# A fused attention and rational feed-forward kernel: its hand-held issue list is replaced by another list of the same tokens

## The chip, the cores and the metric

The program runs on one core of one Trainium2 chip. The metric is the time of the program on the device in microseconds (us), a median over several runs. The engines named here are TensorE (PE in the rows; PEld is its weight load), VectorE (DVE), ScalarE (ACT), GpSimd (POOL) and SyncE (SP), which issues most of the DMA transfers. Each engine runs its own instructions in the order in which the program was written, and waits for the others by semaphores.

## The reference

The first half is an attention between 512 rows of `x` and 32 states, in both directions, for 8 batches and 8 heads of width 64. The result of both directions is one list of 4,352 tokens (8 batches of 512 + 32) of width 512, which goes through a feed-forward layer whose activation is a quotient of two polynomials. All of it is float32.

```python
scores = scale * np.matmul(x, state.transpose(0, 1, 3, 2))      # softmax over 32 states
xread = np.matmul(a, state)
scores2 = scale * np.matmul(state, x.transpose(0, 1, 3, 2))     # softmax over 512 rows
sread = np.matmul(a2, x)
...
h = x @ w_in                                                     # 512 -> 2048
P = a[0] + a[1] * h + a[2] * h2 + a[3] * h3
Q = 1.0 + np.abs(b[0]) * np.abs(h) + np.abs(b[1]) * h2
g = P / (Q + 1e-06)
return (g @ w_out).astype(np.float32)                            # 2048 -> 512
```

## The kernel before

The work is cut into 72 iterations: iteration n takes batch n // 8 (9 "batches": the 8 real ones with 512 rows each, and a last one, n = 64 to 71, with the 256 rows that `sread` made, so half as wide) and the slice n % 8 of the hidden width (256 of 2048 columns). The product of `xread` with `w_in` is folded: the small matrix state times w_in is formed once (tokens `X`, function `extra`, line 695, small tiles of 64 x 32), split into a high and a low float32r part, and multiplied with the softmax weights `a` (token `F`, function `front`, line 785). A float32 product is made of float32r products of high and low parts: three for `F`, and for the output (function `mm`, line 857) two with the high part of g (`mh`) and one with the low part (`ml`).

One iteration has these steps: `F` writes h into one of two PSUM banks that a ring shares (TensorE); `FC` and `FB` make two linear forms of h (ScalarE, lines 797 and 804); `mu`, `po`, `qd` (VectorE, lines 808, 812, 818) read h from PSUM and build both polynomials; `qa`, `ln`, `ex` (ScalarE, lines 824, 894, 904) make the reciprocal of the denominator as the exponential of a logarithm; `g1` (VectorE, line 829), which needs `ex`, writes the high part of g, and `g2`, `g3` (lines 835, 841) with `gl` (GpSimd, line 848) the low part. `mh` and `ml` add to four output banks, which `fl` copies out after 8 iterations and `os` stores. For n of 8 to 63 the folded matrix comes back from DRAM: `lm` loads it (SyncE), `fs` rounds it (ScalarE, line 740), `ft` takes the rest (GpSimd, line 744). The attention of the next batch (`scores`, `tr1`, `row_max`, `e2_T`, `e2_copy`, `sread` and others) runs between the iterations.

In the first 100 us the weights come in as 64-bit words and are turned into float32: `lr` loads a half (SyncE, buffers `raw` and `raw_w`), `cp` and `jr`, `jl` convert it (ScalarE line 300, VectorE lines 309 and 320). `lx` loads the next piece of `x`, `lc` the six coefficients, `ls` the states, and `pre` puts ScalarE's table set in place.

Which engine does what is fixed by these tokens. The order of every engine's work is set by the list `ORDER` alone: the program walks through it from front to back and calls the function of each token, and no scheduler changes that order afterwards.

```python
with tc.manual_schedule():
    for name, args in tokens:
        ops[name](*args)
...
"pre": lambda: nc.scalar.preload_act_table_set("natural_log_exp_and_others"),
"gl": lambda n: fourth(n, nc.gpsimd),
"gv": lambda n: fourth(n, nc.vector),
```

Of the kernel before, what the change touches and what calls it, by code (L numbers as in the profile page):

```python
# [23 lines left out]
    "lx ls:0:2 lc pre lx scores0:0 scores0:1 sc_copy0:0 sc_copy0:1 row_T0:1 col_max:0 row_T0:0 lr:0:0 "  # L24
    "cp:0:0 lr:0:1 jr:0 cp:0:1 row_max0:0 lr:1:0 ls:2:8 cp:1:0 jl:0 X:1 row_max0:1 row_sub0:1 "
    "row_exp0:1 X:0 row_sub0:0 row_exp0:0 XA:1 lr:1:1 cp:1:1 lr:3:0 jr:1 X:2 row_sum0:0 row_norm0:0 "
    "col_scale:0 col_exp:0:0 e2_T0:0 XA:0 fh:0 row_sum0:1 col_exp:0:1 lr:2:0 fo:0 XA:2 a_T0:0 a_hi0:0 "
    "row_norm0:1 jl:1 a_T0:1 lr:2:1 a_hi0:1 cb cv X:4 lr:4:0 lr:4:1 cp:2:0 cp:2:1 a_lo0:0 lr:3:1 XA:4 "
    "a_lo0:1 F:0:0 jr:2 F:0:1 jl:2 fh:1 cp:3:0 fo:1 F:1:0 lx F:1:1 lx cp:4:0 b0a jr:3 col_eps:0 "
    "cp:3:1 jr:4 FB:0 FC:0 jl:3 wh:3 wl:3:0 lr:5:0 wl:3:1 lr:5:1 FB:1 qd:0 qa:0 ln:0 ex:0 mu:0 qd:1 "  # L30
    "po:0 ws:1 e2_T0:1 e2_copy0:0 e2_copy0:1 sread:0:0 sread:0:1 cp:5:0 jr:5 cp:5:1 FC:1 g1:0 qa:1 "
    "mh:0:2 xs:1 g2:0 col_norm:0 sr_copy:0 g3:0 xs:0 lr:7:0 lr:7:1 ln:1 sr_T:0 sr_fin:0 cp:4:1 ws:0 "
    "ex:1 mu:1 po:1 X:5 XA:5 gl:0 jl:5 wh:5 wl:5:0 jl:4 lr:8:0 g1:1 X:8 XA:8 fh:2 cp:7:0 cp:7:1 "
    "mh:0:0 ml:0:0 fo:2 lr:6:0 lr:6:1 xs:5 jr:7 lr:9:0 xs:2 X:9 lr:8:1 g2:1 xs:4 jl:7 wl:5:1 XA:9 "
    "F:2:0 F:2:1 FC:2 FB:2 X:6 cp:6:0 lr:11:0 g3:1 lr:9:1 mh:0:1 jr:6 XA:6 xs:6 ml:0:1 qd:2 cp:6:1 "
    "jl:6 wh:7 qa:2 mu:2 po:2 gl:1 mh:0:3 mh:1:3 ws:2 ln:2 ex:2 ml:1:0 X:12 g1:2 XA:12 fh:3 wl:7:1 "
    "fo:3 xs:8 ml:0:2 cp:8:0 cp:8:1 cp:9:0 cp:9:1 ml:0:3 mh:1:0 jr:9 X:10 XA:10 ml:1:1 lr:10:0 F:3:0 "
    "F:3:1 FC:3 X:16 g2:2 wl:7:0 mh:2:2 jr:8 xs:9 FB:3 XA:16 mh:1:1 lr:11:1 xs:12 jl:9 ws:3 xs:10 "
    "wh:9 g3:2 jl:8 lr:10:1 mh:2:0 gl:2 fh:4 qd:3 qa:3 ln:3 mu:3 mh:1:2 ex:3 mh:2:3 ml:1:2 fo:4 "
    "lr:12:0 lr:12:1 X:13 po:3 g1:3 XA:13 xs:13 wl:9:0 X:14 XA:14 xs:14 cp:11:0 cp:11:1 jr:11 g2:3 "  # L40
    "wl:9:1 ml:2:2 cp:10:0 jr:10 cp:10:1 F:4:0 F:4:1 FC:4 ml:1:3 jl:11 FB:4 g3:3 gl:3 cp:12:0 mh:2:1 "
    "X:20 fh:5 XA:20 lr:13:0 wh:11 lr:13:1 jl:10 mh:3:3 xs:16 qd:4 fo:5 qa:4 xs:20 ml:2:3 mh:3:1 ln:4 "
    "ex:4 F:5:0 lr:14:0 F:5:1 FC:5 ml:3:2 cp:12:1 mu:4 po:4 ws:4 X:17 XA:17 lr:14:1 wl:11:1 wl:11:0 "
    "cp:13:0 jr:13 g1:4 jr:12 lx lx ml:3:1 ml:3:0 g2:4 g3:4 mh:3:2 cp:13:1 FB:5 X:21 XA:21 xs:21 "
    "jl:12 qd:5 qa:5 ln:5 ml:3:3 mh:4:1 mh:4:0 mh:4:3 ws:5 cp:14:0 mu:5 mh:3:0 jr:14 ex:5 po:5 jl:13 "
    "cp:14:1 g1:5 X:25 XA:25 gl:4 scores:1:0 scores:1:1 sc_copy:1 wh:13 ml:2:0 jl:14 ml:4:3 ml:4:0 "
    "wl:13:1 xs:17 g2:5 X:29 col_max:1 X:24 XA:29 fh:6 wl:13:0 ml:2:1 ml:4:1 lr:15:0 tr1:1 mh:4:2 "
    "wh:14 xs:25 col_scale:1 fo:6 F:6:0 col_exp:1:0 lr:15:1 row_max:1 cp:15:0 cp:15:1 F:6:1 g3:5 "
    "wl:14:0 mh:5:2 XA:24 gl:5 row_sub:1 FB:6 qd:6 X:28 row_exp:1 ml:4:2 row_sum:1 row_eps:1 "
    "row_norm:1:0 xs:29 jr:15 mh:5:1 row_norm:1:1 XA:28 col_exp:1:1 fh:7 lm:8 mh:5:3 xs:28 ml:5:3 "  # L50
    "FC:6 fs:8 qa:6 ln:6 fo:7 mh:5:0 lw:0 mu:6 po:6 ws:7 xs:24 ml:5:0 F:7:0 tr2:1 ex:6 g1:6 g2:6 "
    "a_hi:1 ml:5:1 ml:5:2 ft:8 jl:15 X:3 F:7:1 wl:14:1 mh:6:1 XA:3 g3:6 FB:7 col_eps:1 lm:10 FC:7 "
    "e2_T:1 mu:7 qd:7 lx lx gl:6 mh:6:2 lw:1 e2_copy:1 mh:6:0 wh:15 wl:15:1 fs:10 wl:15:0 sread:1:0 "
    "sread:1:1 col_norm:1 sr_copy:1 mh:6:3 ml:6:1 sr_T:1 ml:6:0 po:7 ml:6:3 qa:7 a_lo:1 lm:9 F:8:0 "
    "ln:7 sr_fin:1 ex:7 g1:7 F:8:1 FC:8 g2:7 ml:6:2 g3:7 mh:7:2 mh:7:1 fs:9 ft:9 mh:7:3 mh:7:0 F:9:0 "
    "FB:8 qd:8 qa:8 xs:3 ln:8 ex:8 F:9:1 FC:9 mu:8 po:8 g1:8 gl:7 ml:7:1 ml:7:2 fl:7:2 ft:10 fl:7:1 "
    "ml:7:3 fl:7:3 g2:8 g3:8 gl:8 F:10:0 F:10:1 FB:9 qd:9 FB:10 FC:10 mh:8:3 lm:12 ml:7:0 fl:7:0 "
    "fs:12 ft:12 lx qa:9 ln:9 lm:11 mh:8:1 fs:11 mh:8:2 ws:6 mu:9 po:9 ml:8:1 ml:8:2 F:12:0 F:12:1 "
    "mh:8:0 os:7:3 ex:9 mu:10 lm:13 qd:10 FB:12 po:10 ml:8:3 g1:9 ml:8:0 mh:9:1 mh:9:3 mh:9:0 ft:11 "
    "g2:9 g3:9 FC:12 F:11:0 F:11:1 mu:12 po:12 qa:10 gl:9 ml:9:1 lm:14 lx ln:10 ex:10 ml:9:2 FC:11 "  # L60
    "g1:10 mh:10:2 mh:10:0 fs:13 mh:10:3 FB:11 mh:10:1 qd:12 qa:12 ln:12 g2:10 ml:9:0 ex:12 X:7 g3:10 "
    "XA:7 qd:11 mh:9:2 qa:11 gl:10 ml:10:1 mu:11 ft:13 po:11 scores:2:0 scores:2:1 ln:11 g1:12 g2:12 "
    "sc_copy:2 tr1:2 ex:11 lw:3 X:15 fs:14 lw:6 mh:12:1 F:13:0 F:13:1 col_max:2 g1:11 XA:15 mh:12:0 "
    "g2:11 g3:11 row_max:2 FC:13 ml:10:3 os:7:2 lw:2 FB:13 mh:12:2 qd:13 ft:14 ml:9:3 lm:16 "
    "col_scale:2 lm:15 fs:15 row_sub:2 mh:11:3 xs:15 X:11 ml:10:2 XA:11 mh:11:0 lw:5 gl:11 g3:12 "
    "mu:13 po:13 row_exp:2 ml:11:2 ml:10:0 qa:13 row_sum:2 row_eps:2 gl:12 mh:12:3 ln:13 ex:13 F:14:0 "
    "F:14:1 FC:14 ml:11:0 ft:15 g1:13 mh:11:1 FB:14 qd:14 fs:16 col_exp:2:0 row_norm:2:0 ml:11:3 "
    "mh:11:2 mu:14 col_exp:2:1 g2:13 g3:13 qa:14 F:15:0 F:15:1 ml:12:1 ml:11:1 mh:13:0 FC:15 ml:12:3 "
    "po:14 lm:17 fs:17 ln:14 ex:14 mh:13:1 row_norm:2:1 tr2:2 mh:13:3 e2_T:2 FB:15 ml:12:2 g1:14 "
    "g2:14 mh:13:2 e2_copy:2 gl:13 ml:13:3 ml:13:2 a_hi:2 a_lo:2 mh:14:2 ml:12:0 ft:16 F:16:0 F:16:1 "  # L70
    "FC:16 FB:16 g3:14 mh:14:3 mh:14:0 lm:18 gl:14 ml:14:3 ml:14:1 lx mu:15 po:15 ml:14:2 qd:15 qa:15 "
# [957 lines left out]
```

## Time and profile before

| what | us |
|---|---|
| median of 3 runs (673.9 to 674.11) | 674.07 |
| the profiled execution | 675.09 |
| its span, first to last instruction | 673.3 |
| TensorE busy in the span | 650.9 |
| VectorE busy in the span | 629.3 |
| ScalarE busy | 521.7 |
| GpSimd busy | 307.8 |

The profiled execution took 1.8 us more than its span, and 1.0 us more than the median. The share of busy time of TensorE counts matmuls from the issue of each to its modelled end, so that two neighbours overlap; how dense they stand is read from the distance between their starts. The granted clock was 0.992 of full speed over the span.

### The profile page before, as it was taken

To read this page: it belongs to the slowest core of one execution; us is meant where nothing else is said; L and a number is where in the kernel's file an instruction comes from. 1 tells how busy PE (TensorE), PEld (TensorE's weight loads), DVE (VectorE), ACT (ScalarE), POOL (GpSimd) and SP (SyncE) were. 2 spreads that over 40 slices of the span, in tenths; PEclk is the share of its full clock that TensorE was granted. 3 is DMA by queue.
4 is the path that set the end of the run, shared out by engine and by line. 5 is a ranking of instruction groups with operands and counts; after the bars stand their busy time and mean duration, and the time that the engine had idled before them with its cause. 6 is when DMAs were issued, how large, how long until landed. Compare 5 with 4: busy or idle time off the path is not lost.

```text
span 673.3 us, 11301 instructions
## 1 busy us (share of the span) xinstructions
PE 650.9 (97%) x4474; PEld 509.5 (76%) x4474; DVE 629.3 (93%) x583; ACT 521.7 (77%) x633; POOL 307.8 (46%) x174
## 2 busy tenths in 40 slices
PE   4699999999999999999999999999999999999997
PEld 2466667877877777878878878778778788788895
DVE  4999999899999898999999999999999999998886
ACT  4989989887978788878687777877786868777473
POOL 0234446534644545363544355443554444544540
PEclk9979999999999999999999999999999999999999
DMA  8979887343066164044232210412220311203301
GB/s 329 373 253 356 297 285 251 110 142 127 17 180 210 48 215 149 29 134 140 85 107 88 91 48 17 139 49 77 95 79 17 125 33 47 64 31 94 91 21 47
DMA packets 30679, 85.67 MB, mean 127 GB/s; under 512 B 3490, under 2 KB 3618, under 8 KB 30626
## 3 DMA queue, kind: packets, MB, share of 16 engines
q1 hardware_dynamic: 30290, 84.56, 36.9%
q8 instruction: 35, 0.57, 0.4%
q10 hardware_dynamic: 336, 0.39, 0.3%
q14 instruction: 18, 0.15, 0.1%
HBM read 57.15 MB, written 27.79 MB: 126 GB/s over the span
## 4 chain that ended last, share of the span: by engine, by line
PE 41%; DVE 34%; ACT 11%; issue 9%; POOL 2%; DMA 1%; SPq 0%; DVEq 0%; POOLq 0%; ACTq 0%
PE h L785 13%; DVE gh L829 7%; DVE C L808 5%; DVE A L818 5%; DVE A L835 5%; DVE C L812 3%; DVE C L841 3%; PE ps_x L695 2%; POOL gl L848 2%; PE o__5821 L857 2%; PE o__5809 L857 2%; ACT A L824 1%; ACT cv_y L300 1%; ACT C L797 1%; DVE aT L500 1%
## 5 line engine op out<-in xcount | busy, mean ns | idle before, releaser
L848 POOL TENSOR_TENSOR gl<-C,L 128x1024 fp32r<-128x1024 f32 (+1 forms) x70 | 176.0, 2516 | 255.1 <-DVE C L841 164.9
L785 PE MATMUL h<-aT,m 128*128 128x512 f32 x768 | 188.8, 392 | 1.3 <-DVE m L731 0.6
L785 PEld LDWEIGHTS h<-aT,m 128*128 128x128 f32 x768 | 142.5, 188 | 37.2 <-DVE m L731 2.3
L829 DVE SCALAR_TENSOR_TENSOR gh<-C,cst,L 128x1024 fp32r<-128x1024 f32 (+1 forms) x72 | 94.4, 1312 | 12.9 <-ACT L L904 9.9
L797 ACT ACTIVATE C<-h,cst 128x1024 f32<-128x1024 f32 (+1 forms) x72 | 83.3, 1157 | 28.1 <-PE h L785 23.2
L804 ACT ACTIVATE A<-h,cst 128x1024 f32<-128x1024 f32 (+1 forms) x72 | 76.8, 1067 | 32.6 <-PE h L785 26.9
L744 POOL TENSOR_TENSOR m<-m_sb,m 128x512 fp32r<-128x512 f32 x56 | 80.1, 1439 | 36.2 <-ACT m L740 20.4
L835 DVE SCALAR_TENSOR_TENSOR A<-A,gh 128x1024 f32<-128x1024 f32 (+1 forms) x72 | 91.5, 1270 | 1.7
L841 DVE SCALAR_TENSOR_TENSOR C<-C,cst,A 128x1024 f32<-128x1024 f32 (+1 forms) x72 | 89.4, 1246 | 1.4
L824 ACT ACTIVATE A<-A 128x1024 f32<-128x1024 f32 (+1 forms) x72 | 72.9, 1013 | 22.9 <-DVE A L818 22.5
L818 DVE SCALAR_TENSOR_TENSOR A<-A,b0a,h 128x1024 f32<-128x1024 f32 (+1 forms) x72 | 86.9, 1215 | 3.4 <-ACT A L804 2.4
L812 DVE SCALAR_TENSOR_TENSOR C<-C,cst,h 128x1024 f32<-128x1024 f32 (+1 forms) x72 | 87.7, 1219 | 1.9
L808 DVE TENSOR_TENSOR C<-C,h 128x1024 f32<-128x1024 f32 (+1 forms) x72 | 82.9, 1152 | 4.2 <-ACT C L797 3.8
L894 ACT ACTIVATE L<-A 128x1024 f32<-128x1024 f32 (+1 forms) x72 | 73.0, 1014 | 5.2 <-POOL gl L848 1.4
L904 ACT ACTIVATE L<-L 128x1024 f32<-128x1024 f32 (+1 forms) x72 | 72.9, 1013 | 1.8
L695 PE MATMUL ps_x<-win_sb,st 64*32 64x256 f32 x1024 | 37.7, 420 | 2.9 <-DVE win_sb L320 2.2
L740 ACT CAST m<-m_sb 128x512 fp32r<-128x512 f32 x56 | 34.0, 615 | 5.1 <-PE h L785 2.2
L695 PEld LDWEIGHTS ps_x<-win_sb,st 64*32 64x32 f32 x1024 | 18.1, 114 | 18.1 <-issue 7.4
L337 POOL TENSOR_TENSOR wo<-cv_r,wo 128x512 fp32r<-128x512 f32 x16 | 21.7, 1378 | 19.6 <-ACT wo L330 19.6
L785 PEld LDWEIGHTS h<-sh,m 128*128 128x128 f32 x192 | 23.9, 191 | 1.6 <-POOL sh L912 0.6
L785 PE MATMUL h<-sh,m 128*128 128x256 f32 x192 | 24.4, 284 | 0.4 <-POOL sh L912 0.4
L490 POOL TENSOR_TENSOR e<-e,rs 128x512 f32<-128x512 f32 x14 | 16.4, 1189 | 17.6 <-DVE rs L484 13.1
(246 smaller groups left out, 1109.1 us busy)
## 6 DMA issues: line engine op xcount, KB each, us to landing
m_sb<-m_dram SPq DMA_DIRECT2D x56, 256.0 KB, 3.0
xT_sb<-in_xT_dram SPq DMA_DIRECT2D x16, 512.0 KB, 4.4
x_sb<-in_x_dram SPq DMA_DIRECT2D x16, 512.0 KB, 6.9
m_dram<-xo SPq DMA_DIRECT2D x16, 512.0 KB, 4.2
win_sb<-w_in_dram SPq DMA_DIRECT2D x16, 512.0 KB, 5.0
out_dram<-o_sb SPq DMA_DIRECT2D x32, 256.0 KB, 3.7
raw<-in_w_in_dram SPq DMA_DIRECT2D x10, 512.0 KB, 7.5
raw_w<-in_w_out_dram SPq DMA_DIRECT2D x8, 512.0 KB, 7.2
```

Source lines behind the costliest of these rows:

```text
L744: nc.gpsimd.tensor_tensor(m[:, 1], MF.pop(n), m[:, 0].bitcast(F32), op=ALU.subtract)
L785: nc.tensor.matmul(h[:, ci * W : (ci + 1) * W], l, r, start=(q == 0), stop=(q == len(seq) - 1),)
L797: nc.scalar.activation(e["C"], e["h"], AF.Identity, scale=cst[:, 3:4], bias=cst[:, 2:3])
L804: nc.scalar.activation(e["A"], e["h"], AF.Abs, scale=cst[:, 5:6])
L808: nc.vector.tensor_tensor(e["C"], e["C"], e["h"], op=ALU.mult)
L812: nc.vector.scalar_tensor_tensor(e["C"], e["C"], cst[:, 1:2], e["h"], op0=ALU.add, op1=ALU.mult)
L818: nc.vector.scalar_tensor_tensor(e["A"], e["A"], b0a, e["h"], op0=ALU.add, op1=ALU.mult)
L824: nc.scalar.activation(e["A"], e["A"], AF.Abs)
L829: nc.vector.scalar_tensor_tensor(e["gh"], e["C"], cst[:, 0:1], e["L"], op0=ALU.add, op1=ALU.mult)
L835: nc.vector.scalar_tensor_tensor(e["A"], e["A"], 1.0 + 1e-6, e["gh"].bitcast(F32), op0=ALU.add, op1=ALU.mult)
L841: nc.vector.scalar_tensor_tensor(e["C"], e["C"], cst[:, 0:1], e["A"], op0=ALU.add, op1=ALU.subtract)
L848: eng.tensor_tensor(e["gl"], e["C"], e["L"], op=ALU.mult)
```

## The change

The list `ORDER` is replaced as a whole. Both lists hold the same 2,335 tokens, each as often, and every function behind them is the same. So each engine does the same operations on the same shapes (574 rows of VectorE's order, 4,474 matmuls), in another order and at other places beside the other engines. Its first lines stand for all of it:

```diff
ORDER = [
-    "lx ls:0:2 lc pre lx scores0:0 scores0:1 sc_copy0:0 sc_copy0:1 row_T0:1 col_max:0 row_T0:0 lr:0:0 "
-    "cp:0:0 lr:0:1 jr:0 cp:0:1 row_max0:0 lr:1:0 ls:2:8 cp:1:0 jl:0 X:1 row_max0:1 row_sub0:1 "
-    "row_exp0:1 X:0 row_sub0:0 row_exp0:0 XA:1 lr:1:1 cp:1:1 lr:3:0 jr:1 X:2 row_sum0:0 row_norm0:0 "
...
+    "lx ls:0:2 lx scores0:0 scores0:1 sc_copy0:0 row_T0:0 sc_copy0:1 col_max:0 lr:0:0 pre row_T0:1 "
+    "row_max0:0 cp:0:0 lr:0:1 cp:0:1 jr:0 row_max0:1 jl:0 row_sub0:1 lr:1:0 cp:1:0 ls:2:8 X:1 "
+    "row_sub0:0 row_exp0:1 lc col_scale:0 row_exp0:0 row_sum0:0 row_norm0:0 lr:1:1 jr:1 cp:1:1 "
...
```

All line numbers after the list are one less in the changed kernel, because the new list has one line less. Three places show what moves.

ScalarE at the start of the program, before: the copies of the first scores out of PSUM (`sT<-ps_sc`), the conversion of the first weights (`cv_y<-raw`), the exponentials of the first softmax (`e`) and the copies of the first folded products (`xo`, `m`).

```order
L259 DMA st<-in_stT_dram 128x256
L915 ACT_TABLE_LOAD
L526 COPY sT<-ps_sc_97 128x512
L526 COPY sT<-ps_sc_98 128x512
L300 ACTIVATE cv_y<-raw 128x512 x3
L566 ACTIVATE e_141<-e_141 128x512 x2
L713 COPY xo_w<-ps_x 128x1024
L300 ACTIVATE cv_y<-raw 128x512
L428 ACTIVATE e_219,r_124<-sT,cm 128x512
L713 COPY xo<-ps_x 128x512
```

The same place of the changed kernel:

```order
L258 DMA st<-in_stT_dram 128x256
L525 ACT_TABLE_LOAD
L525 COPY sT<-ps_sc_95 128x512
L525 COPY sT<-ps_sc_96 128x512
L914 ACT_TABLE_LOAD
L299 ACTIVATE cv_y<-raw 128x512 x3
L565 ACTIVATE e_134<-e_134 128x512 x2
L299 ACTIVATE cv_y<-raw 128x512
L427 ACTIVATE e_181,r_122<-sT,cm 128x512
L712 COPY xo_w<-ps_x 128x1024
```

The token `pre` now stands behind the two copies, so that a load of a default table set is put ahead of the first copy and the load of `pre` between the copies and the first conversion: two table loads instead of one. The fourth conversion and one exponential stand ahead of the first copy of a folded product, which was ahead of them.

SyncE's queue at the start, before: it issues the loads of `xT`, of the coefficients (`row`), of the weights (`raw`, `raw_w`), of the states (`st`) and of `x`.

```order
L364 DMA xT_sb<-in_xT_dram 128x1024
L246 DMA row<-in_cab_dram 1x6
L364 DMA xT_sb<-in_xT_dram 128x1024
L282 DMA raw<-in_w_in_dram 128x1024 x3
L259 DMA st<-in_stT_dram 128x768
L282 DMA raw<-in_w_in_dram 128x1024
L288 DMA raw_w<-in_w_out_dram 128x1024
L282 DMA raw_w<-in_w_in_dram 128x1024 x2
L282 DMA raw<-in_w_in_dram 128x1024 x2
L288 DMA raw_w<-in_w_out_dram 128x1024
L367 DMA x_sb<-in_x_dram 128x1024 x2
L288 DMA raw<-in_w_out_dram 128x1024 x2
```

The same place of the changed kernel:

```order
L363 DMA xT_sb<-in_xT_dram 128x1024 x2
L281 DMA raw<-in_w_in_dram 128x1024 x3
L258 DMA st<-in_stT_dram 128x768
L245 DMA row<-in_cab_dram 1x6
L281 DMA raw<-in_w_in_dram 128x1024
L281 DMA raw_w<-in_w_in_dram 128x1024 x2
L281 DMA raw<-in_w_in_dram 128x1024
L287 DMA raw_w<-in_w_out_dram 128x1024 x2
L281 DMA raw<-in_w_in_dram 128x1024
L287 DMA raw<-in_w_out_dram 128x1024 x2
L366 DMA x_sb<-in_x_dram 128x1024 x2
```

The coefficients are loaded behind the states instead of between the two pieces of `xT`, and the two loads of `x` stand behind a pair of weight loads into the ring `raw` that they were ahead of.

ScalarE around iteration 22, before: `qa` and `ln` of the iteration (lines 824 and 894), the copy `e2T` of the attention of batch 3 (line 470), and `ex` (line 904), which `g1` of the iteration needs; `xo` are copies of folded products.

```order
L713 COPY xo<-ps_x 128x1024 x2
L824 ACTIVATE A<-A 128x1024
L894 ACTIVATE L<-A 128x1024
L470 COPY e2T<-ps_e_2624 128x1024
L904 ACTIVATE L<-L 128x1024
L713 COPY xo<-ps_x 128x1024 x2
```

The same iteration of the changed kernel:

```order
L796 ACTIVATE C<-h,cst 128x1024
L469 COPY e2T<-ps_e_2583 128x1024
L823 ACTIVATE A<-A 128x1024
L893 ACTIVATE L<-A 128x1024
L712 COPY xo<-ps_x 128x1024 x2
L903 ACTIVATE L<-L 128x1024
```

The copy `e2T` has moved ahead of `qa`, and two copies of folded products now stand between `ln` and `ex`. On VectorE the list puts eight tokens between `qd` and `g1` of this iteration (`row_sum:3 row_eps:3 col_eps:3 mu:22 po:22 g2:20 g3:20 tr2:3`) where there were two (`po:22 g3:20`).

## Rows read from the trace of the kernel before

**Rows 1.** The page, busy time of each engine, share of the span, instructions.
```profile
PE 650.9 (97%) x4474; PEld 509.5 (76%) x4474; DVE 629.3 (93%) x583; ACT 521.7 (77%) x633; POOL 307.8 (46%) x174
```
**Rows 2.** Windows: us, then busy time of each engine, granted clock, DMA share, GB/s.
```profile
100.00:660.00 560.00, 557.42 (x3474) 447.58 (x3473) 535.82 (x481) 435.27 (x514) 273.68 (x147) 1.00 0.29 95
```
**Rows 3.** Chain that ended last, and timeline of TensorE: start us, us, what.
```profile
300.14 2.72 PE h L785 x12
...
97.11 2.12 PE L785 MATMUL h<-aT,m 128*128 128x512 f32 x7
...
667.92 1.09 PE L857 MATMUL o__5809<-wo,gl 128*128 128x512 f32 x4
...
669.05 0.69 DVE L876 COPY o_sb<-o__5809 128x512 f32<-128x512 f32 x1 [1.75 <-PE o__5809 L857]
```
**Rows 4.** Waits of VectorE: waited for, total us, times, longest.
```profile
DVE gh L829 <- ACT L L904: 9.9, 9, 2.9
DVE cm L398 <- ACT sT L526: 9.0, 1, 9.0
```
**Rows 5.** Groups by form: line, engine, out<-in, count | busy us, mean ns | idle before.
```profile
L829 DVE SCALAR_TENSOR_TENSOR gh<-C,cst,L 128x1024 fp32r<-128x1024 f32 x64 | 87.2, 1362 | 11.6 <-ACT L L904 9.9 <-PE o__4160 L857 0.6
L835 DVE SCALAR_TENSOR_TENSOR A<-A,gh 128x1024 f32<-128x1024 f32 x64 | 84.8, 1326 | 1.6
L812 DVE SCALAR_TENSOR_TENSOR C<-C,cst,h 128x1024 f32<-128x1024 f32 x64 | 81.8, 1278 | 1.6
L904 ACT ACTIVATE L<-L 128x1024 f32<-128x1024 f32 x64 | 67.9, 1061 | 1.6
L695 PE MATMUL ps_x<-win_sb,st 64*32 64x256 f32 x1024 | 37.7, 420 | 2.9 <-DVE win_sb L320 2.2 <-ACT srT L641 0.6
```
**Rows 6.** Timeline of iteration 22: start us, us, engine, line, idle before in brackets.
```profile
253.98 1.06 ACT L894 ACTIVATE L<-A 128x1024 f32<-128x1024 f32 x1
...
255.69 1.01 ACT L470 COPY e2T<-ps_e 128x1024 f32<-128x1024 f32 x1 [0.64 <-PE ps_e L407]
...
256.60 1.06 ACT L904 ACTIVATE L<-L 128x1024 f32<-128x1024 f32 x1
...
257.69 1.77 DVE L829 SCALAR_TENSOR_TENSOR gh<-C,cst,L 128x1024 fp32r<-128x1024 f32 x1 [2.87 <-ACT L L904]
```
**Rows 7.** Timeline of the start.
```profile
1.17 1.28 ACT L915 ACT_TABLE_LOAD   x1 [1.17 <-PEq L1011]
1.20 0.34 SPq L246 DMA_DIRECT2D row<-in_cab_dram  x1
1.59 0.36 SPq L364 DMA_DIRECT2D xT_sb<-in_xT_dram  x1
...
7.92 1.07 ACT L526 COPY sT<-ps_sc 128x512 f32<-128x512 f32 x2 [5.46 <-PE ps_sc L514]
8.87 1.36 ACT L300 ACTIVATE cv_y<-raw 128x512 f32<-128x512 f32 x2
...
15.43 0.99 ACT L713 COPY xo_w<-ps_x 128x1024 f32<-128x1024 f32 x1
```
**Rows 8.** Loads of x: their issue, their landing, and the product that reads them.
```profile
12.29 1.18 SPq L367 DMA_DIRECT2D x_sb<-in_x_dram  x2
...
DMA to landing us min/median/max: 11.1/11.3/11.5
...
32.95 2.21 PE L618 MATMUL ps_sr<-x_sb,e2T 128*32 128x64 f32 x64 [4.83 <-ACT e2T L605]
```
**Rows 9.** A VectorE instruction beside GpSimd, and lines 829, 835 by min/median/max ns.
```profile
402.32 3.26 POOL L848 TENSOR_TENSOR gl<-C,L 128x1024 fp32r<-128x1024 f32 x1 [1.27 <-DVE C L841]
...
403.23 3.43 DVE L829 SCALAR_TENSOR_TENSOR gh<-C,cst,L 128x1024 fp32r<-128x1024 f32 x1
...
L829 DVE SCALAR_TENSOR_TENSOR gh<-C,cst,L x72: 742/1280/3433, 32.7 to 662.9; 128x1024 fp32r<-128x1024 f32 x64, 128x512 fp32r<-128x512 f32 x8
L835 DVE SCALAR_TENSOR_TENSOR A<-A,gh x72: 677/1224/2320, 34.0 to 665.0; 128x1024 f32<-128x1024 f32 x64, 128x512 f32<-128x512 f32 x8
```

335 rows, old and new, of the table ORDER are left out of this document.

## The prediction

> **What bounds the kernel now.** I read first the busy time of the engines [rows 1]: TensorE 97% and VectorE 93% of a span of 673.3 us, so two engines are full at once and neither can be called the bound from the page alone. The windows then say where they are full [rows 2]: from 100 to 660 us VectorE is busy for 535.82 of 560 us, so it stands still for only 24.2. TensorE's busy time can't be read in this way, because its matmuls overlap; I take the distance of their starts instead. Twelve products of `F` in a row take 2.72 us [rows 3], 0.227 us for each 512 columns. Iteration 6 begins at 97.11 and the last matmul ends at 669.0 [rows 3], 571.9 us later. By the list, behind that point stand 252 `mh` of four, 253 `ml` of two and 116 full `F` of six products, 2,210 in all, or 501 us; the 192 half-wide products, at 0.12 us each, are an estimate of 23 more. 47.9 us are left, and in them lie 13 of the 32 visits of `X` (13/32 of 37.7 us [rows 5], 15.3) and the small attention products. So TensorE waits for less than 32.6 us in 572; I estimate half of it, 16. Any reordering behind the first 100 us can win no more than that, and the most it can win on VectorE is 24.2.
>
> The waits of VectorE come next [rows 4]. The largest is the start, 9.0 us until the first scores are copied. The next is `g1` (line 829), which waits 9.9 us in 9 places for `ex`. The longest of these places is iteration 22 [rows 6]: the copy `e2T` stands between `ln` and `ex` on ScalarE, waits 0.64 us for TensorE, and `g1` starts 2.87 us after VectorE became free.
>
> Last I looked at VectorE's durations beside GpSimd. At 403.23 a `g1` takes 3.43 us, because a `gl` that began at 402.32 ran until 405.58 [rows 9]; the median of line 829 is 1.28 us. Over the kernel such holds cost it (1362 - 1280) ns x 64 = 5.2 us, and line 835 (1326 - 1224) ns x 64 = 6.5 us [rows 5, 9].
>
> **The change part by part.** No instruction is added on TensorE, VectorE, GpSimd or SyncE, and one on ScalarE, a table load. Everything else is order.
>
> *The start.* The load of the coefficients leaves the place between the two loads of `xT`; the second of these is issued at 1.20 instead of 1.59 [rows 7], and with it the copies of the first scores, now at 7.92, come 0.39 us earlier. Behind the copies ScalarE then has the second table load. The one row of before lasts 1.28 us [rows 7], hidden in the wait for the first loads; now it is in the open. So the conversion of the first weights, at 8.87 before, begins 1.28 - 0.39 = 0.9 us later. Queued behind it on ScalarE are the exponentials of the first softmax and the copies of the first folded products, whose PSUM banks the third visit of `X` waits for. The first of these copies, at 15.43 [rows 7], also falls behind one conversion and one exponential, some 1.5 us of ScalarE. Against that, VectorE does the first subtractions about 0.4 us earlier, and one of the transposes of `e2` leaves TensorE's way to the first `F`. I take +0.5 us for the first `F` and all behind it; the ends are -0.4 (the load hidden, the earlier start kept) and +1.3 (the load in the open). The coefficients themselves, issued some 3 us later, are needed by a product at about 20 us, so that is hidden.
>
> The Trainium skill, "ScalarE: Activation LUTs", section "What ACT_TABLE_LOAD costs", gives 1283 ns for the load, which the row confirms, but another 1380 ns for a drain at each switch to a different set, which no row here can show, since ScalarE then idled. By the page the start would cost 1.4 us more than by the row, and the forecast would be 673.7.
>
> The two loads of `x` stand behind a pair of weight loads that wait for a buffer of the ring `raw`; that comes free when the fourth conversion and its `jr` are done. The conversion now stands ahead of the copy that began at 15.43 [rows 7], and with the table load and `jr` I put the release at 18 us. Their landing took 11.3 us from an issue at 12.29 [rows 8]; from 18 it would be at 29.3. The product that reads them starts at 32.95 and waits then for `e2T` [rows 8]. So this costs nothing, covered by 3.6 us of that wait; without the cover each microsecond is one of TensorE's.
>
> *The waits for `ex`.* For each iteration I compared, in both lists, the VectorE work between `qd` and `g1` with the ScalarE work from `qa` to `ex` (three steps of 1.06 us [rows 5] with what stands between them, plus 0.3 us for three handovers). Where ScalarE's sum is larger, `g1` must wait for the difference. Before, this adds up to 12.0 us in ten iterations; the trace has 9.9 [rows 4], so a count is worth 0.83. It names the trace's long place, 22, with 1.9 us. In the new list it adds up to 9.6 us in twelve iterations: 22 is gone, since eight tokens now stand between `qd` and `g1`, and the largest are 62 (2.1), 58 (1.3), and 2, 8, 18, 23 and 59 with about 1 each. The difference is 2.4 x 0.83 = -2.0 us on VectorE.
>
> *The waits for a PSUM bank.* The same count for the ring of two banks (the last reader of a bank on VectorE, then `F` with 1.36 us, then `FB` or `FC`, against the VectorE work until its next `qd` or `mu`) gives 1.6 us in five places before and 0.3 in one after: -1.3 us.
>
> *How much of it reaches the end.* VectorE gains 3.3 us. None of it counts if TensorE is the bound everywhere, all if VectorE is. Behind 100 us VectorE's 24.2 us of standing still and TensorE's 16 are of one size, and each `F` waits for VectorE's banks and each `mh` for its `g1`; a wait of VectorE for 1 us or more delays both. I take 0.7, -2.3 us.
>
> *The end.* In both lists the last low part is made on VectorE, six products, a copy (at 669.05 [rows 3]) and the store follow: no change.
>
> The sum is 675.09 + 0.5 - 2.3 = 673.3 us for an execution like the profiled one. That one lay 1.0 us above the median, so the median becomes 672.3. With the ends of both terms (-0.4 - 3.3 and +1.3 + 0) the case runs from 670.4 to 675.4; what of it lies below 672.7 is my forecast, the rest the first rival.
>
> **The rivals.** *No change.* TensorE stands dense enough that VectorE's shorter waits change nothing, or the start costs its upper end, +1.3 us. For it: the lead of VectorE over TensorE, counted as work in front of each `F`, has its tightest places within 2 us of each other in the two lists. Against it: `g1` at iteration 22 held up both engines. Time: 675.09 + 0.5 - 1.0 = 674.6; or 675.09 + 1.3 - 2.3 - 1.0 = 673.1.
>
> *A larger gain.* TensorE's own waits, which my counts don't see, shrink too: half of the estimated 16 us would give 664; a third, 667 to 669. For it speaks that the whole list was laid again; against it, that they consist of many waits of about 0.1 us.
>
> *Slower by collisions with GpSimd.* Every `g1`, `g2` and `g3` that comes upon a running GpSimd instruction may be held until that ends, as at 403.23 [rows 9]. The new list sets `ft` and `gl` at other times, and no count of mine tells how these meet. If the 11.7 us of holds on lines 829 and 835 become half as long again, VectorE loses 5.9, of which 4.1 reach the end: 672.3 + 4.1 = 676.4. It decides from 40% more on (4.5 us on VectorE). The Trainium skill, "SBUF — State Buffer", section "Who interferes with whom", says that a VectorE instruction with two SBUF inputs and a GpSimd instruction that reads SBUF exclude each other for the whole instruction, whichever came first; the rows agree.
>
> *Slower by the loads of `x`.* If weights and `x` share the DMA engines so that `x` lands after 33 us, `sread` and all TensorE work queued behind it wait. Landing at 36 adds 3 us: 675.3. It decides from 35 on.
>
> **How the numbers follow.** A difference of 0.2%, 1.35 us, is about what a measurement of this kernel can tell from no change. Forecast 0.32 (670.4 to 672.7); larger gain 0.14; no change 0.28; collisions 0.17; loads of `x` 0.09. So faster 0.46, same 0.28, slower 0.26. The range goes from 667.5, a third of TensorE's waits won, to 677.5, the collisions with a little more: it leaves out less than 2 in 10. The forecast's own range is 670.4 to 672.7.
>
> **What would show it.** A second table load of 1.28 us at about 8.6, with the first conversion at 9.8 or so; the first `F` at 22.2 instead of 21.7; `sread` not waiting for a DMA; VectorE's wait for `ex` near 8 us in all, none at iteration 22, and waits of 1 to 2 us at 58 and 62; means of lines 829 and 835 near 1.36 and 1.33 us. I would be wrong if these means rose by 0.07 us, if `sread` waited for `x_sb`, or if VectorE's waits fell while the time stood still.

## The result and the profile after

| what | before | after |
|---|---|---|
| median, us | 673.99 (673.19 to 674.11, 4 runs) | 667.87 (667.36 to 668.84, 4 runs) |
| the profiled execution, us | 675.09 | 668.84 |

The ratio of the new kernel to the old is 0.9913, with a 95% interval of 0.9896 to 0.9931: 6.1 us faster (4.7 to 7.0). The direction was forecast, but the forecast was a gain of 1.7 us, and the time lies below its own range (670.4 to 672.7). It lies inside the whole range by 0.4 us, and only because that range reaches down to a rival's price. The profiled executions lie 1.1 and 1.0 us above their medians, and both stood at half the clock for 10.2 to 10.3 us near 40 us, so the two traces can be subtracted: 6.25 us.

Line numbers of the new kernel are those of before less one. The page of the new kernel, busy time of each engine and the shares of the chain that ended last:

```profile
PE 645.3 (97%) x4474; PEld 509.2 (76%) x4474; DVE 624.2 (94%) x583; ACT 521.8 (78%) x634; POOL 306.0 (46%) x174
...
PE 88%; DVE 5%; ACT 4%; issue 1%; DMA 1%; POOL 0%; SPq 0%; POOLq 0%; DVEq 0%; ACTq 0%
```

The same chain line of the kernel before:

```profile
PE 41%; DVE 34%; ACT 11%; issue 9%; POOL 2%; DMA 1%; SPq 0%; DVEq 0%; POOLq 0%; ACTq 0%
```

This is the plainest difference of the two pages. Before, the chain went back and forth between TensorE and VectorE; now it stays on TensorE for 88% of the span. With the same work, VectorE is busy 5.1 us less [rows 1], so its instructions have become shorter. In the same 560 us as [rows 2] it is busy for 536.32 us in the new kernel, so it stands still there as long as before (24.2 us, now 23.7):

```profile
100.00:660.00 560.00, 558.46 (x3498) 453.54 (x3483) 536.32 (x488) 435.73 (x515) 271.10 (x147) 1.00 0.28 96
```

Where did 6.25 us come from? In both kernels the first product of `F` 6 marks the same place of the start: 97.11 us before [rows 3], 96.73 after, so 0.4 us were won by then. Behind it I summed what the distance from the start of each product of `F`, `mh` and `ml` to the next start on TensorE is above 0.227 us (0.120 us behind the half-wide ones), where this is over 0.015 us: 14.0 us at 108 places before, 8.6 us at 73 places after. That is 5.4 us of the remaining 5.9. These places are of four kinds:

| kind of place | before | after |
|---|---|---|
| the product waits for a result that another engine has just finished | 20 places, 5.6 us | 4 places, 2.1 us |
| the product right behind such a wait (0.07 to 0.12 us each) | 20 places, 2.1 us | 4 places, 0.4 us |
| the step to a product of another shape (0.09 us each) | 22 places, 2.0 us | 22 places, 2.0 us |
| single delays of 0.02 to 0.11 us at products whose input came earlier | 46 places, 4.3 us | 43 places, 4.0 us |

So the gain is in the waits for other engines, 16 fewer, each with a delay of some 0.1 us at the next product: 5.2 of the 5.4 us. The many single delays of 0.1 us stayed as they were. Before, the 20 waits are for the low part `gl` (7 places, with the products behind them 2.6 us), for the high part `gh` (4 places, 1.8 us), for `a_lo` (3 places, 1.0 us) and for others (6 places, 2.3 us); after, one for `gl` (0.7 us), one for `gh` (0.3 us) and two others (1.6 us).

The view of TensorE's waits shows few of them. It counts from the modelled end of the product before, which lies 0.39 us behind its start, and lists what is left above 0.15 us. Behind 97 us it shows of the kernel before

```profile
PE o__4731 L857 <- DVE gh L829: 0.5, 1, 0.5
PE h L785 <- POOL sh L912: 0.4, 1, 0.4
PE o__4169 L857 <- POOL gl L848: 0.4, 1, 0.4
PE h L785 <- DVE A L818: 0.3, 1, 0.3
PE o__1511 L857 <- POOL gl L848: 0.2, 1, 0.2
PE h L785 <- DVE aT L500: 0.2, 1, 0.2
```

and of the new kernel

```profile
PE h L784 <- DVE C L811: 1.1, 1, 1.1
PE o__4162 L856 <- POOL gl L847: 0.4, 1, 0.4
```

By this view alone the waits have hardly become less (2.0 and 1.5 us).

The waits of VectorE in the new kernel:

```profile
DVE cm L397 <- ACT sT L525: 8.4, 1, 8.4
DVE gh L828 <- ACT L L903: 8.1, 10, 1.3
DVE A L817 <- ACT A L803: 4.6, 4, 2.1
DVE C L807 <- ACT C L796: 2.2, 6, 0.7
```

The wait for `ex` fell from 9.9 to 8.1 us and its longest place from 2.9 to 1.3 [rows 4], and the wait for `C` from 3.8 to 2.2. But the wait for `A` rose from 2.4 to 4.6. Over all waits above 0.15 us behind the start VectorE stands still for 23.1 us before and 23.0 after. So VectorE lost its long waits for `ex` and got others in their place; the waits for `C` and `A` together rose from 6.2 to 6.8.

What became shorter on VectorE are instructions that had been held by GpSimd, by form, in the new kernel:

```profile
L828 DVE SCALAR_TENSOR_TENSOR gh<-C,cst,L 128x1024 fp32r<-128x1024 f32 x64 | 86.3, 1349 | 11.0 <-ACT L L903 8.1 <-ACT e L473 1.2 <-PE o__2181 L856 0.3
L834 DVE SCALAR_TENSOR_TENSOR A<-A,gh 128x1024 f32<-128x1024 f32 x64 | 81.4, 1273 | 1.3
L499 DVE TENSOR_TENSOR aT<-a,aT 128x1024 fp32r<-128x1024 f32 x7 | 8.6, 1233 | 0.0
L401 DVE TENSOR_SCALAR cm<-cm 128x2 f32<-128x2 f32 x8 | 3.6, 446 | 0.0
```

Lines 829 and 835 had means of 1362 and 1326 ns [rows 5]; they are now 1349 and 1273. Line 500, `a_lo`, went from a mean of 1665 ns to 1233. The last row is the exception: the scaling of the column maxima, two columns wide, had a mean of 184 ns in the kernel before and has 446 here, because one of the eight was held. Taking for every VectorE instruction what it lasted above the median of its form, where that is over 0.1 us, I count 21.4 us of holds at 30 places before and 17.1 at 35 after; at each of these places a GpSimd instruction was running.

### The profile page after: what moved, and what is told of

The parts are those of the page before. It is cut to its first block, busy times and chain, and to the rows that moved or that the text cites. A ratio compares the mean times of both kernels' runs of the same rounds, so it can differ in the third digit from the quotient of the medians.

```text
span 667.0 us, 11303 instructions
## 1 busy us (share of the span) xinstructions
PE 645.3 (97%) x4474; PEld 509.2 (76%) x4474; DVE 624.2 (94%) x583; ACT 521.8 (78%) x634; POOL 306.0 (46%) x174
## 4 chain that ended last, share of the span: by engine, by line
PE 88%; DVE 5%; ACT 4%; issue 1%; DMA 1%; POOL 0%; SPq 0%; POOLq 0%; DVEq 0%; ACTq 0%
PE h L784 27%; PE ps_x L694 4%; PE o__494 L856 2%; PE o__522 L856 2%; PE o__547 L856 2%; PE o__2200 L856 2%; PE o__411 L856 2%; PE o__2960 L856 2%; PE o__2181 L856 2%; PE o__5846 L856 2%; PE o__1512 L856 2%; PE o__1507 L856 2%; PE o__2193 L856 2%; PE o__2220 L856 2%; PE o__1502 L856 2%; PE o__4763 L856 2%
## 5 line engine op out<-in xcount | busy, mean ns | idle before, releaser
L847 POOL TENSOR_TENSOR gl<-C,L 128x1024 fp32r<-128x1024 f32 (+1 forms) x70 | 173.3, 2477 | 247.3 <-DVE C L840 169.7
L784 PE MATMUL h<-aT,m 128*128 128x512 f32 x768 | 186.2, 391 | 1.1 <-DVE C L811 1.1
L828 DVE SCALAR_TENSOR_TENSOR gh<-C,cst,L 128x1024 fp32r<-128x1024 f32 (+1 forms) x72 | 94.8, 1318 | 11.4 <-ACT L L903 8.1
L796 ACT ACTIVATE C<-h,cst 128x1024 f32<-128x1024 f32 (+1 forms) x72 | 83.3, 1157 | 24.2 <-PE h L784 18.2
L743 POOL TENSOR_TENSOR m<-m_sb,m 128x512 fp32r<-128x512 f32 x56 | 77.7, 1398 | 51.6 <-ACT m L739 47.2
L834 DVE SCALAR_TENSOR_TENSOR A<-A,gh 128x1024 f32<-128x1024 f32 (+1 forms) x72 | 87.4, 1215 | 1.5
L712 ACT COPY xo<-ps_x 128x1024 f32<-128x1024 f32 (+1 forms) x24 | 20.8, 872 | 6.6 <-PE ps_x L694 5.2
```

Source lines behind the costliest of these rows:

```text
L743: nc.gpsimd.tensor_tensor(m[:, 1], MF.pop(n), m[:, 0].bitcast(F32), op=ALU.subtract)
L784: nc.tensor.matmul(h[:, ci * W : (ci + 1) * W], l, r, start=(q == 0), stop=(q == len(seq) - 1),)
L796: nc.scalar.activation(e["C"], e["h"], AF.Identity, scale=cst[:, 3:4], bias=cst[:, 2:3])
L828: nc.vector.scalar_tensor_tensor(e["gh"], e["C"], cst[:, 0:1], e["L"], op0=ALU.add, op1=ALU.mult)
L834: nc.vector.scalar_tensor_tensor(e["A"], e["A"], 1.0 + 1e-6, e["gh"].bitcast(F32), op0=ALU.add, op1=ALU.mult)
L847: eng.tensor_tensor(e["gl"], e["C"], e["L"], op=ALU.mult)
```

## The experiments

All were read against these theories. **P** is the prediction: VectorE's shorter waits reach the end at 0.7, and the start costs 0.5 us. **T**: TensorE is the bound behind 100 us, and its own waits have become shorter. **G**: VectorE is the bound, and GpSimd holds it less often. From the second group's result came **J** (both engines are full together, and time comes back only where both are relieved) and **L** (a chain through a third engine sets the pace).

### The new order up to a place, the old one behind it

```diff
 # in words, for k = 413, 947, 1447:
-ORDER = old
+ORDER = new[:k] + (old without the entries of new[:k])
```

`e1_to100`: 

> The new order for the first 413 entries of the list (to about 100 us), the old order behind them. Theory P (VectorE's shorter waits pass through to the end, and the second table load costs something at the start): +0.5 us against before. Theory T (TensorE is the bound behind 100 us, and the gain is the fall of its own waits): -0.5, the lead that F:6 already has. Theory G (VectorE is held less often by GpSimd): -0.3.

`e1_to260`: 

> The new order for the first 947 entries (to about 260 us), the old one behind them. P: 0 to -0.5 (the wait of iteration 22 is mended, but the start costs 0.5). T: -3.0 to -3.5, since TensorE's lost time falls by 1.4 and 1.7 us in 100 to 200 and 200 to 300 us and its start leads by 0.5. G: -2.2 (holds of 7.1 us before and 4.9 after up to there).

`e1_to395`: 

> The new order for the first 1447 entries (to about 395 us), the old one behind them. P: -1. T: -4.5 to -5. G: -4 (holds of 10.3 us before and 6.3 after up to there), or more where the holds at 395 to 560 us fall out otherwise.

| kernel | median, us | ratio to before, 95% interval | us against before, by the ratio |
|---|---|---|---|
| e1_to100 | 676.83 | 1.0032 (1.0020 to 1.0045) | +2.2 |
| e1_to260 | 674.52 | 1.0004 (0.9995 to 1.0013) | +0.3 |
| e1_to395 | 670.14 | 0.9939 (0.9927 to 0.9952) | -4.1 |

None of the three fits all: the first is slower than each of them put it (P is nearest), the second lies just above P's end of 0, and the third is G's figure (-4), with T near it and P (-1) far off. Behind the seam, where the two lists meet, the traces keep a constant distance to the kernel before (within 0.05 us from iteration 18 on in the first), so each kernel's total is settled at its seam. Two things besides the order stand in these totals. The three traces were at half the clock for 13.7 us in the start, against 10.2 of the kernel before, and have `F` 6 at 97.45 to 97.90 us instead of 97.11. And a seam has a price of its own: in e1_to100 the low-part products of iteration 6 come right behind their input, and the waits of TensorE at 97 to 135 us, where the same view lists none for the kernel before, are

```profile
PE o__522 L858 <- POOL gl L849: 0.6, 1, 0.6
PE o__522 L858 <- POOL wo L338: 0.2, 1, 0.2
```

What can be read is the difference of two such kernels. Between 260 and 395 us 4.4 us are won (674.52 to 670.14), more than any theory put there; a part of it may be the better seam. From 260 to 400 us of the new kernel TensorE's delays sum to 1.3 us, against 3.3 before, and VectorE's holds to 1.4 against 3.2.

### One table load at the start

```diff
-scores0:0 scores0:1 sc_copy0:0 row_T0:0 sc_copy0:1 col_max:0 lr:0:0 pre row_T0:1 ...
+pre scores0:0 scores0:1 sc_copy0:0 row_T0:0 sc_copy0:1 col_max:0 lr:0:0 row_T0:1 ...
```

`e1_onetab`: 

> The new list with the first conversion's tokens put back ahead of the first score group, so that ScalarE loads one table at the start instead of two. P: -0.4 to -1.3 against the new kernel, if the second load cost what the prediction put to it. T: within 0.5 of the new kernel, since its first products already start 1.0 us earlier than before with the second load.

The token that the edit moves is `pre`, which loads the table; the conversion itself stays in its place.

Measured: 669.64 us (667.70 to 669.86), ratio to before 0.9921 (0.9907 to 0.9935), so no gain against the new kernel (0.9913) is to be seen. The start of the new kernel:

```profile
7.24 1.07 ACT L525 COPY sT<-ps_sc 128x512 f32<-128x512 f32 x2 [4.79 <-PE ps_sc L513]
...
8.34 1.28 ACT L914 ACT_TABLE_LOAD   x1
...
9.63 1.78 ACT L299 ACTIVATE cv_y<-raw 128x512 f32<-128x512 f32 x3
...
11.29 1.21 DVE L319 SCALAR_TENSOR_TENSOR win_sb<-cv_y,cv_r 128x1024 int32<-128x1024 int32 x1
```

and of the kernel with one load:

```profile
9.49 0.66 ACT L300 ACTIVATE cv_y<-raw 128x512 f32<-128x512 f32 x1 [0.56 <-DMA raw<-in_w_in_dram]
10.78 0.66 ACT L300 ACTIVATE cv_y<-raw 128x512 f32<-128x512 f32 x1 [0.63 <-DMA raw<-in_w_in_dram]
11.33 1.22 DVE L320 SCALAR_TENSOR_TENSOR win_sb<-cv_y,cv_r 128x1024 int32<-128x1024 int32 x1
```

Without the second load ScalarE waits for the weights to land, and the weights are joined at 11.33 instead of 11.29. The first `F` starts at 20.78 us, against 20.72 with two loads. The load of 1.28 us lies in the wait for a transfer; it costs nothing, as T expected.

### Less work for one engine, in twelve iterations

```diff
 # shortened: the lines that change, put together
 def mm_lo(n, t):                          # e2_..._lessPE
+    if t < 2 and n in (12, 17, 21, 26, 30, 34, 38, 42, 46, 50, 54, 58): return
     mm(n, t, (("gl", 0),))
 def second(n):                            # e2_..._lessDVE, the same n
-    e["A"], e["A"], 1.0 + 1e-6, e["gh"]
+    e["A"][:, :320], e["A"][:, :320], 1.0 + 1e-6, e["gh"][:, :320]
```

`e2_before_lessPE`: 

> The kernel before without the low-part products of two of four output tiles in twelve iterations spread from 12 to 58 (24 visits of two products left out, 24 x 0.453 = 10.9 us of TensorE; the output lacks these products). Theory T (TensorE is the bound): -10 to -11 us against before. Theory P (VectorE's time passes through at 0.7): -3, the rest. Theory G (VectorE is the bound, and its holds by GpSimd are what changed): 0 to -1.

`e2_before_lessDVE`: 

> The kernel before with the second product of VectorE (the line with 1.0 + 1e-6) over 320 of 1024 columns in the same twelve iterations (about 0.8 us of VectorE each, 9.8 us in all; what these columns should hold is left out). G: -9 to -10 against before. P: -7. T: 0 to -2.

`e2_after_lessPE`: 

> The new kernel with the same 24 visits of TensorE left out. T: -10 to -11 against the new kernel (657). P: -3. G: 0 to -1.

`e2_after_lessDVE`: 

> The new kernel with the same twelve second products of VectorE over 320 of 1024 columns. G: -9 to -10 against the new kernel (658). P: -7. T: 0 to -2, less than in the kernel before, since TensorE waits less.

| kernel | median, us (range) | us against the same order whole |
|---|---|---|
| e2_before_lessPE | 675.40 (674.5 to 676.5) | +1.1 |
| e2_before_lessDVE | 671.05 (670.66 to 671.8) | -3.3 |
| e2_after_lessPE | 666.51 (664.24 to 668.65) | -1.4 (by the ratios to before -2.0) |
| e2_after_lessDVE | 666.93 (666.75 to 667.14) | -0.9 (by the ratios -1.6) |

The new order itself was not run again beside these kernels, so its two rows are given in both ways. VectorE's busy time fell by 8.1 and 8.5 us. So in the old order 0.4 of it reached the end (interval of the ratio 0.9936 to 0.9968, 2.2 to 4.3 us), and of 10.9 us of TensorE nothing: that kernel is even slower (1.0009 to 1.0029). In the new order neither relief can be told from nothing: the intervals of both ratios overlap that of the new kernel. There is also a second change in both of them. A scaling of column maxima that is held for 2.39 us at 445 us in the new kernel (last group below) takes 0.16 us here, so a gain of up to 2.1 us need not come from the relief. T, P and G all fall as stated. The waits of TensorE in e2_before_lessPE show where its time went:

```profile
PE h L786 <- DVE aT L501: 1.4, 2, 1.0
PE h L786 <- POOL sh L915: 1.1, 1, 1.1
PE h L786 <- DVE C L813: 1.0, 3, 0.4
PE o__4141 L858 <- DVE gh L830: 0.8, 1, 0.8
```

and the shares of its chain that ended last:

```profile
DVE 35%; PE 17%; issue 7%; ACT 5%; POOL 2%; DVEq 0%; POOLq 0%; ACTq 0%
```

This chain can be followed back only to 224.50 us, so its shares are of two thirds of the span. In the stretch from 240 us on, which both traces cover, TensorE has 41% of the chain before and 26% here, VectorE 39% and 51%. With less to do, TensorE comes to its next input earlier and stands there: its delays, counted as above, grow from 14.0 to 24.6 us, almost the 10.9 that were taken out, and the waits for `gl` among them from 7 places to 12. VectorE does not profit either. It stands still for 19.7 us instead of 23.1, but its holds by GpSimd grow from 21.4 to 24.7. In e2_before_lessDVE it is the other way: VectorE's wait for `ex` grows from 9.9 to 12.3 us, and the chain moves to TensorE (71%).

### Iteration 22 mended, and both engines relieved

```diff
-qa:22 ln:22 ml:19:1 gl:20 e2_T:3 e2_copy:3 ml:21:2 ex:22 g1:22
+e2_T:3 e2_copy:3 qa:22 ln:22 ml:19:1 gl:20 ml:21:2 ex:22 g1:22
 ...
 # and both edits of the group before, for n in (30, 34, 38, 42, 46, 50, 54, 58)
```

`e3_before_22both`: 

> The kernel before with two edits that are read apart by their place. First, the transposes and the copy of e2T of the third softmax stand ahead of the second absolute value of iteration 22, so that the wait of g1 there is shorter. Theory P (VectorE's wait passes through at 0.7): -1.3 us at iteration 29. Theory J (TensorE and VectorE are full together, and time comes back only where both are relieved): 0 to -0.3 there, since TensorE lost nothing near 266 us. Second, from iteration 30 on, in eight iterations both the 0.9 us of TensorE's low-part products and the 0.8 us of VectorE's second product are left out. J: -5 to -7 more by the end (0.7 to 0.9 at each place), though each alone gave almost nothing. Rival L (a third engine or a fixed chain of waits sets the pace): 0 to -2.

Measured: 674.08 us, ratio 0.9997 (0.9988 to 1.0007). The first edit did not do what it was for. ScalarE now stands at the copy for longer:

```profile
254.54 1.01 ACT L471 COPY e2T<-ps_e 128x1024 f32<-128x1024 f32 x1 [2.29 <-PE ps_e L408]
255.45 1.06 ACT L825 ACTIVATE A<-A 128x1024 f32<-128x1024 f32 x1
256.60 1.06 ACT L899 ACTIVATE L<-A 128x1024 f32<-128x1024 f32 x1
...
258.78 1.28 DVE L830 SCALAR_TENSOR_TENSOR gh<-C,cst,L 128x1024 fp32r<-128x1024 f32 x1 [4.64 <-ACT L L909]
259.70 2.56 PE L786 MATMUL h<-aT,m 128*128 128x512 f32 x10 [1.26 <-ACT xo L714]
```

The wait of `g1` grew from 2.87 us [rows 6] to 4.64, by 1.8, and the product of `F` behind it, which waits for a copy queued behind `ex` on ScalarE, slipped from 0.7 us ahead of the kernel before to 0.7 us behind. So a longer wait at this place is paid with about 0.8 of its length. What a shorter one would bring, this kernel does not tell. From iteration 30 on, both reliefs together brought 1.8 us (from 0.8 behind to 1.0 ahead at iteration 71), not 5 to 7, as L expects. But the trace shows that they did not meet: `g2` of iteration 34 runs at 369.1, the two `ml` left out ran at 377.3 and 387.8 in the kernel before, and in between VectorE had already given its lead back:

```profile
369.13 0.49 DVE L837 SCALAR_TENSOR_TENSOR A<-A,gh 128x320 f32<-128x320 f32 x1
...
372.46 1.22 ACT L798 ACTIVATE C<-h,cst 128x1024 f32<-128x1024 f32 x1
...
373.76 1.22 DVE L809 TENSOR_TENSOR C<-C,h 128x1024 f32<-128x1024 f32 x1 [0.62 <-issue]
```

It stands for 0.62 us at the next product that needs `C`, which ScalarE makes from TensorE's `F` and ends at 373.68. So J in its strict form, a relief at the same place, was not tried, and it stays open against L.

### A shorter `gl` on GpSimd

```diff
-eng.tensor_tensor(e["gl"], e["C"], e["L"], op=ALU.mult)
+w = e["N"] // 4 if eng is nc.gpsimd else e["N"]
+if w < e["N"]:
+    eng.memset(e["gl"][:, w:].bitcast(F32), 0.0)
+eng.tensor_tensor(e["gl"][:, :w], e["C"][:, :w], e["L"][:, :w], op=ALU.mult)
```

`e3_before_lessPOOL`: 

> The kernel before with GpSimd's gl over a quarter of its columns, the rest set to zero ahead of it without reading anything (the low parts of these columns are left out). VectorE should be held less (21.7 us before). Theory G: the holds cost most of what the new order won, so this comes to 667 to 669 and the two orders are then within 2 us. Theory J: VectorE alone relieved, 671 to 673, and the two orders stay 4 to 6 us apart.

`e3_after_lessPOOL`: 

> The new kernel with the same shorter gl. G: 666 to 667, hardly faster than the new kernel, since its holds already cost little. J: 665 to 667, and 4 to 6 us below the kernel before with the same edit.

Measured: 669.70 us in the old order, ratio 0.9939 (0.9925 to 0.9954), and 667.07 in the new, 0.9893 (0.9876 to 0.9909). The old order wins 4.4 us, the new one 0.8 (1.3 by the ratios), and of the 6.1 us between them 2.6 are left. That lies between G (667 to 669, at most 2 apart) and J (671 to 673, 4 to 6 apart). In the old order, by form:

```profile
L836 DVE SCALAR_TENSOR_TENSOR A<-A,gh 128x1024 f32<-128x1024 f32 x64 | 83.2, 1300 | 1.6
L830 DVE SCALAR_TENSOR_TENSOR gh<-C,cst,L 128x1024 fp32r<-128x1024 f32 x64 | 82.8, 1293 | 12.9 <-ACT L L908 11.5 <-PE o__4202 L861 0.3
...
L852 POOL TENSOR_TENSOR gl<-C,L 128x256 fp32r<-128x256 f32 x64 | 57.9, 904 | 130.7 <-DVE C L842 96.7 <-ACT C L798 10.3 <-DVE r L457 7.1
L851 POOL MEMSET gl<- 128x768 f32 x64 | 47.4, 741 | 123.7 <-PE o__1552 L861 14.8 <-PE o__595 L861 11.6 <-PE o__3590 L861 10.8
```

VectorE's holds fell from 21.4 to 11.4 us there, and from 17.1 to 13.5 in the new order. More than half of what the new order wins is thus had in the old one by a shorter `gl`. The edit does two things, though: it holds VectorE less, and it makes the last step to the low-part products shorter (0.90 us instead of 2.61 in the mean). TensorE's delays in front of the first low-part products fell from 1.8 to 0.2 us with it, and all of its delays from 14.0 to 10.4. Of these 3.6 us, 2.3 are the waits for `gl` with the products behind them. The edit does not say which of the two counts.

### One hold taken out of the new kernel

```diff
-mu:44 qa:44 ln:44 ex:44 col_scale:6 po:44
+col_scale:6 mu:44 qa:44 ln:44 ex:44 po:44
```

`e3_after_mend6`: 

> The new kernel with the scaling of the column maxima of the sixth softmax one place earlier on VectorE, ahead of mu of iteration 44 instead of behind ex, so that it no longer meets the gl that began at 445.02 and held it 2.39 us. J: -1.3 to -2.1 against the new kernel (TensorE's two waits of 1.28 and 0.56 us at 448.8 and 456.2). P: -1.6 (0.7 of the hold). If other collisions take its place: 0.

The place in the new kernel:

```profile
445.02 2.40 POOL L847 TENSOR_TENSOR gl<-C,L 128x1024 fp32r<-128x1024 f32 x1 [2.53 <-PE o__4153 L856]
445.06 2.39 DVE L401 TENSOR_SCALAR cm<-cm 128x2 f32<-128x2 f32 x1
...
447.36 1.27 DVE L811 SCALAR_TENSOR_TENSOR C<-C,cst,h 128x1024 f32<-128x1024 f32 x1
...
448.77 1.61 PE L784 MATMUL h<-aT,m 128*128 128x512 f32 x6 [1.12 <-DVE C L811]
449.75 1.27 DVE L828 SCALAR_TENSOR_TENSOR gh<-C,cst,L 128x1024 fp32r<-128x1024 f32 x1
```

The same order with one table load (e1_onetab) has the same collision, so it belongs to the order and not to one execution:

```profile
445.82 2.40 DVE L402 TENSOR_SCALAR cm<-cm 128x2 f32<-128x2 f32 x1
```

With the mend:

```profile
442.91 0.16 DVE L402 TENSOR_SCALAR cm<-cm 128x2 f32<-128x2 f32 x1
...
444.00 2.42 POOL L848 TENSOR_TENSOR gl<-C,L 128x1024 fp32r<-128x1024 f32 x1 [2.54 <-PE o__4153 L857]
444.23 1.28 DVE L812 SCALAR_TENSOR_TENSOR C<-C,cst,h 128x1024 f32<-128x1024 f32 x1
...
446.48 2.88 PE L785 MATMUL h<-aT,m 128*128 128x512 f32 x12
446.62 1.28 DVE L829 SCALAR_TENSOR_TENSOR gh<-C,cst,L 128x1024 fp32r<-128x1024 f32 x1
```

`gl` starts 1.02 us earlier in the mended kernel, which is a lead from its start that has nothing to do with the mend; `g1` behind it starts 3.13 us earlier. The difference, 2.1 us, is what the mend won, and it is kept to the end (the first product of `F` 71 starts 3.15 us earlier). The median is 667.21 us (665.75 to 668.57), ratio 0.9901 (0.9885 to 0.9918): 0.7 us below the new kernel's (0.8 by the ratios), and the intervals of the two overlap. The trace with the mend is that of the fastest of its four runs, the trace of the new kernel that of the slowest of its four. So the trace shows the gain of 2.1 us in its place, and the medians do not yet show a kernel faster than the new one.

## Why the prediction was right and wrong

The time was right by luck: the forecast's mechanism, shorter waits of VectorE, did not bring it, and the range held the result only through a rival with a chance of 0.14.

**The start.** Forecast +0.5 us; measured -1.0 at the first `F` (20.72, against 21.68 before) and -0.4 at iteration 6. The table load and the conversion stood near where they were put, at 8.34 and 9.63 us. The term was mis-sized because the load was counted in the open: it lies in the wait for the weights' transfer (e1_onetab). With that cost gone, the weights are joined at 11.29 us instead of 11.72, and the transposes `ps_e`, which took TensorE 0.87 us at 18.36 before, no longer stand ahead of the first `F`. The drain of 1380 ns that the Trainium skill ("ScalarE: Activation LUTs", "What ACT_TABLE_LOAD costs") adds does not show: the conversion follows the load's end within 0.02 us. The forecast by it, 673.7, falls with it.

**The loads of x.** Right: issued at 17.10 (18 forecast), landed after at most 9.5 us, and the product that reads them waits for `e2T`, not for a transfer.

**The waits for `ex` and for a bank.** The first is near in size: -1.8 us (-2.0 forecast), though iteration 22 still waits 1.0 us and no place waits longer than 1.3. The second fails. The count of banks took in the waits of both `mu` (for `C`) and `qd` (for `A`) and gave -1.3; those for `C` fell by 1.6, but those for `A` rose by 2.2. In sum VectorE stands still as long as before (23.1 and 23.0 us), so the 3.3 us that it was to gain in waits were not there.

**How much of it reaches the end.** This step failed too, "I take 0.7". It took one number for all places. The relief of VectorE in twelve iterations came through at 0.4 in the old order and can't be told from nothing in the new; a wait made longer by 1.8 us at iteration 22 cost 0.8 of it; a hold of 2.2 us taken away at 445 us gave 2.1 in the trace. Those two are places where a product of TensorE was standing behind the delay, or came to. That elsewhere the time went into the next wait is argued; it was looked at only at iteration 34.

**A larger gain.** This rival came true in its time (667 to 669) and its place: TensorE's own delays fell by 5.4 of 14.0 us, 0.39 of them. The third that it named is near by luck, though, because the 16 us were taken for waits. Of the 14.0 us only 7.7 are waits for other engines with the products behind them, and of these two thirds went (to 2.5). The argument against the rival, many waits of about 0.1 us, holds for the rest: the single delays stayed at 4.3 and 4.0 us. What shrank are 20 waits of 0.03 to 0.66 us. The two traces show the low parts further from their products: the first high-part product of an iteration stands 1.80 us behind the end of its `g1` in the median of 67 before and 2.13 after, the first low-part product 0.92 and 1.60 us behind its `gl` on GpSimd (65), and those that stand less than 0.3 us behind are 22 before and 13 after. That the larger distance is the cause is argued, not shown by a run.

**Collisions with GpSimd.** The mechanism was right and its sign was not: the holds fell by 4.3 us in sum. The Trainium skill ("SBUF — State Buffer", "Who interferes with whom"), which the prediction named for this, also says that a VectorE instruction in a two-port mode excludes GpSimd, and that a `tensor_scalar` can enter such a mode. The held `cm` agrees: the 128x2 instruction that began 0.04 us behind a `gl` lasted as long as it. In which mode it ran, no row shows.

**What stays open.** Whether TensorE waits less in the new order because VectorE is held less or because the products of `gl` and `gh` stand further behind them; whether both engines relieved at one place would bring the sum (not tried); what the single delays of 0.1 us are; and what of the 2.6 us that remain with a shorter `gl` belongs to which engine.

## What to carry to other kernels

Where two engines are both busy for 93% or more and hand over to each other in each iteration, a microsecond saved on one of them is not worth a fixed share: look up, at its own place, which instruction of the other engine is waiting there. A view of waits shows only a part of what such a kernel loses on TensorE (2.0 us here, where the starts show 7.7). Sum the distances between the starts of equal matmuls, and keep apart the places where another engine's result had just come: those a new order can change, and the rest stayed nearly the same here whatever the order. Count a load or table switch as exposed only after looking for the transfer that would be waited for anyway.

## What had not been expected of the hardware

The granted clock near 40 us differs from one execution to the next and moves all that follows. Windows of the new kernel (the clock, as a share of 2.4 GHz, is the third column from the end):

```profile
36.00:39.00 3.00, 2.34 (x33) 0.76 (x33) 2.96 (x4) 2.50 (x4) 2.38 (x1) 0.50 0.19 78
...
42.00:45.00 3.00, 3.00 (x19) 2.45 (x12) 2.18 (x3) 2.04 (x4) 1.62 (x2) 0.80 0.97 268
```

and of e3_after_mend6, which has the same order up to there:

```profile
36.00:39.00 3.00, 1.69 (x35) 0.64 (x33) 2.96 (x3) 3.00 (x8) 1.83 (x1) 1.00 0.22 87
```

In both, TensorE had been busy for under a third of 27 to 33 us. In the first it then stood at 1.2 GHz from 32.9 to 43.2 us, in the second only from 32.3 to 35.7. `F` 6 came at 96.73 us in the one and at 95.34 in the other. This lead of 1.4 us, of which 1.0 is left at 440 us, is larger than the difference of their medians; it is the scatter in which effects below one microsecond vanish. The 14 traces of this case bear it out: with 3.4 to 3.5 us at 1.2 GHz `F` 6 comes at 95.3 to 95.7 us (two traces), with 6.9 at 96.2 (one), with 10.2 to 10.3 at 96.3 to 97.1 (five), and with 13.7 at 97.3 to 97.9 (six).

The order has a part in this. All six traces with 13.7 us begin with the new list. The kernel before had a mean clock of 0.992 or more in all its runs with the experiments; the kernels that begin with the new list had 0.990 or less in 33 of 47. For the kernel before, runs at 0.992 lie some 0.7 us above those at 0.994 to 0.997. So the new start seems to lose by the clock a part of what it wins; no run was made to show this. Behind the start, by contrast, the program repeats itself to 0.05 us, so that one trace tells a local change that the medians do not.
